# Scores of a seventh pair of heads from unsplit fp32 q and k in a one-core attention and spectral-mixing kernel

## The chip, the cores and the metric

One core of a Trainium2 chip runs the whole program. The metric is device time in microseconds (us), the median of several runs. Lower is better.

## The reference, cut to what matters

Four batches, 12 heads, 448 positions, head size 64, so 768 channels. Causal attention feeds a block that turns its output by learned phases, mixes it along the sequence and projects it.

```python
scores = scale * np.matmul(q, k.transpose(0, 1, 3, 2))      # causal mask, softmax
x = np.matmul(attn, v)                                      # (4, 448, 768) after a transpose
theta = x @ w_theta
zr, zi = x * np.cos(theta), x * np.sin(theta)
y = np.einsum('ts,bsd->btd', w_tok_r, zr) + np.einsum('ts,bsd->btd', w_tok_i, zi)
u = x + y
out = u + np.maximum(u @ w_ch, 0.0)
```

## The kernel before

All matrix products run on TensorE (PE). Most operands are fp32 numbers split into a high and a low fp32r part (a rounded copy and what the copy lost), and a product is the sum of two or three fp32r matmuls. The alternative, one fp32 matmul on the unsplit numbers, shows in the trace as two records per matmul.

Heads are worked in 24 pairs, 6 per batch, pair 0 to 23. For each pair:

- `load_pair` (L383) brings q, k and v. For the first `NQ` pairs (L386) it loads k once into a `kk` buffer and each head's q into one half of the partitions of a zero-padded buffer `QZ` (tiles named `qz`; QZ is a buffer of the rings `zh` and `zl`, two halves used by even and odd pairs). For the other pairs it loads k and q whole (`kr`, `qr`), makes the high part (`copy`, L402, executed by L334 on ScalarE, ACT, or L336 on VectorE, DVE), takes the low part (`alu`, L403, executed at L342), and sends per head two `kk` pieces and two `qs` pieces through DMAs from SBUF to SBUF (L409 and L411).
- `head` (L423) computes per head four score tiles `s` of 448, 336, 224 and 112 columns (matmul L441 for the first NQ pairs, L444 twice for the others), a DVE pass that masks, scales and takes the row minimum (L447), the exponential with its row sums on ACT (L450), and ten 112x112 transposes on PE (L474), which DVE or ACT copies out of PSUM (`p`, L336 or L334).
- After the second head of the pair the row sums are inverted (L457, L458), transposed by PE (L459) into the single PSUM buffer of the ring `xo`, copied out by DVE (`rs`, L460), written to DRAM (`rd`) and read back spread over 64 partitions twice (`rb`). PE then multiplies p and v (L491) into `xo`, and DVE multiplies by `rb` into `xT` (L494). Since `xo` has one buffer, the transposed sums of a pair wait for L494 of the pair before, and the product of p and v waits for L460.

`batch` (L500) follows for each batch: x is split (`xs`, L519 to L523), theta is computed in eight groups of matmuls (L540) into the three PSUM buffers of the ring `m`, DVE takes the fraction of each group (`R`, L562), which frees the buffer, ACT takes sines and cosines, `prep` transposes x and builds the split operands `zh` and `zl`, and `mix` does the sequence mixing (`y`, L620). `project` (L664) and `pair` (L695) do the last product for batches 1 and 2, and for 3 and 0 together. Weights are loaded and split in stages of their own (`weight`, L373, and `decode`, L352): `w_theta` goes to `wth`, `w_tok` to `wtk` during the attention of the first batches.

The order of all instructions is made before the program runs. Each operation has a due time computed from the table `KN` (L22), and `Plan.order` (L97) walks a simple model of the engines: a free engine takes the ready operation with the earliest due time for which buffers are free. Operations with several possible engines (DVE, ACT, GpSimd, which is POOL here) go to the one that is free in the model. So a change of the numbers in KN moves instructions on every engine. All DMAs are issued by one queue, SP, in order; an issue that waits for its data or a buffer holds up all later ones.

```python
def load_pair(pr):
    b, p = divmod(pr, NP)
    t0 = tau(2 * pr)
    if pr < KN["NQ"]:
        kp = buf("kk", [128, 2, S])
```

Of the kernel before, what the change touches and what calls it, by code (L numbers as in the profile page):

```python
# [18 lines left out]
MAGIC = 12582912.0  # L19


KN = dict(S0=-2520.8995, P0=3914.469, P1=7056.6972, V=0.0339, TL=0.8835, RL=-0.0438, SL=7631.8556, SH=2896.8187,  # L22
          LD=2238.5021, LW=-1908.5532, M0=-3353.0467, MR=1.7842, MR2=-0.0229, W0=15032.9046, WT=3030.4005,
          W1=2485.321, WK=2746.2629, E0=-8178.3792, CR=419.9564, O0=2180.1597, OR=0.4535, X0=-265.4206, NS=1, PR=2,
          AE=15377.7073, BB=-1728.1953, AP=5033.1175, AQ=2425.1203, XT=3, NQ=6, WP=2, NW=4, EX=0.4254, PORT=1,
          DW=1450, DE=150, DB=250.0, SL2=0, UL=1823.0792, UD=372.3266, SB=51637.6906, SC=462.9947, XL=-895.2931,
          TS=0.2508, SW=3360.6242, WQ=2)


class Buf:  # L30
# [11 lines left out]
class Plan:  # L42
# [12 lines left out]
    def op(self, eng, dur=None, fn=None, r=(), w=(), lat=None, pr=None, table=None, after=(), port=("POOL",), pen="AP", mode="m"):  # L55
        o = Op()
        o.pen = KN[pen]
        o.port = port
# [38 lines left out]
    def order(self):  # L97
# [3 lines left out]
        def delay(a, b):  # L101
            if b == "PE":
                return 0 if a == "PE" else (310 if a == "POOL" else 365)
            if a == "PE":
                return 197
            if a == "POOL":
                return 102 if b == a else 75
            return 157 if b == "POOL" else 130
# [6 lines left out]
        def turn(a, b):  # L115
            if a == b:
                return 0
            if b == "x":
                return 146
            if a == "x":  # L120
                return 150 if b == "t" else 101
            return 17 if a == "t" and b == "m" else 0
# [28 lines left out]
        while done < len(self.ops):  # L151
# [10 lines left out]
            for e in free:  # L162
# [3 lines left out]
                for o in ready[e]:  # L166
                    if port > t and e in o.port and KN["PORT"]:
                        continue
                    if best is not None and (o.pr > best.pr + KN["SW"] or turn(last[0], o.mode)):
                        continue  # L170
# [23 lines left out]
                if o.wire:  # L194
                    wire = max(wire, fin + KN["DW"]) + o.wire
                    end = wire + KN["DE"]
                out.append((t, o.idx, o))
# [10 lines left out]
                for x in o.succ:  # L208
                    x.n -= 1
                    x.ready = max(x.ready, end + max(delay(e, a) for a in x.alts) + KN["SL2"])  # L210
                    if not x.n:
# [8 lines left out]
def attention_moe_kernel(  # L220
# [42 lines left out]
    def buf(ring, shape, dtype=F32, name=None):  # L263
        def make():
            if ring in ("s", "t", "xo", "m"):
                pool = psum
            elif ring in in_moe:
                pool = moe
            elif ring == "xT":
                pool = xpool  # L270
            elif ring == "rd":
                pool = dram
            elif ring == "ub":
                pool = o_pool[0]
            else:
                pool = apool
            return pool.tile(shape, dtype, tag=ring, name=name or ring, bufs=rings[ring])
        return P.buf(ring, make)
# [35 lines left out]
    def dma(fns, nbytes, r=(), w=(), pr=None, after=(), half=False):  # L314
        def run():
            for f in fns():
                nc.sync.dma_start(out=f[0], in_=f[1])  # L317
        n = nbytes[0]
        o = P.op("SP", 530 if n == 1 else 615.0 * n, run, r, w, lat=0, pr=pr, after=after)
        o.wire = nbytes[1] / KN["DB"]  # L320
        return o
# [3 lines left out]
    def copy(n, o, i, r, w, psum=False, engs=("DVE", "ACT"), after=()):  # L325
        alts = []
        if not psum and P.now <= KN["AE"]:
            engs = tuple(engs) + ("POOL",)
# [10 lines left out]
    def alu(n, o, a, b, op, r, w, engs=("POOL", "DVE"), after=(), pool=False):  # L339
        if P.now > KN["AE"] and not pool:  # L340
            engs = ("DVE",)
        P.op([(e, gp(n) if e == "POOL" else dv(n), lambda e=e: ENG[e].tensor_tensor(out=o(), in0=a(), in1=b(), op=op))  # L342
              for e in engs], r=r, w=w, after=after, port=("POOL", "DVE"))

    def tau(s):
        return KN["S0"] + KN["P0"] * min(s, H) + KN["P1"] * max(s - H, 0)

    def boost(h):
        return KN["BB"] * max(0, h % H - (H - 3)) / 2
# [23 lines left out]
    def weight(src, n, t, i, key, t0, pool):  # L373
        raw = buf("R", [128, 2 * n], I32, "raw")
        z = buf("C", [128, 2, n], F32, "zw")
        dma(lambda: [(raw.t, src.bitcast(I32))], (1, 1024 * n), [], [raw], pr=t0 - KN["LW"])
        P.now = t0
        decode(raw, z, n, lambda: t[:, i, 0], lambda: t[:, i, 1], (key, i), pool)
# [4 lines left out]
# [5 lines that stand above are left out]
            dma(lambda: [(kp.t[:, 0], k[b, p])], (1, 229376), [], [kp], pr=t0 - KN["LD"] - 50000)  # L388
            for hh in range(2):
                own = slice(64 * hh, 64 * hh + 64)  # L390
                qz, i = QZ[hh], pr % 2
                dma(lambda qz=qz, own=own, i=i: [(qz.t[own, i], q[b, p, own])], (1, 114688), [], [(qz, i)],
                    pr=t0 - KN["LD"] + hh - 49999)
                KS[2 * pr + hh], QS[2 * pr + hh] = kp, (qz, i)
        else:
            t1 = t0 - KN["SL"]
            parts = []
            for n, (ring, src) in enumerate((("kr", k), ("qr", q))):
                y = buf(ring, [128, 2, S], F32R)
                dma(lambda y=y, src=src: [(y.t[:, 1].bitcast(F32), src[b, p])], (1, 229376), [], [(y, 0), (y, 1)], pr=t1 - KN["LD"])  # L400
                P.now = t1 + 300 * n
# [12 lines left out]
        vs = buf("vs", [TQ, NJ, 2, D])  # L414
        dma(lambda: [(vs.t, v[b, p])], (1, 229376), [], [vs], pr=t0 - KN["LD"] + 1000)
        VS[pr] = vs
# [6 lines left out]
    def head(h):  # L423
# [42 lines left out]
        for n, js in enumerate(((2,), (3, 1), (0,))):  # L466
            P.now = t0 + per * (KN["TL"] + (1.5, 3, 4)[n] * KN["TS"]) - boost(h)
            pt = buf("t", [TQ, S])
# [366 lines left out]
    for i in range(NTK):  # L835
        weight(w_tok[i], S, wtk, i, bwtk, tau(H) + KN["W1"] + KN["WK"] * i, KN["WP"])
    n_att = len(P.ops)
# [140 lines left out]
```

## Time and profile before

| | |
|---|---|
| median of 3 runs | 484.84 us (483.5 to 486.14) |
| the profiled execution | 482.89 us |
| its span in the profile | 481.1 us |
| busy in the span: PE | 467.7 us (97%) |
| DVE | 396.6 us (82%) |
| ACT | 281.9 us (59%) |
| POOL | 17.6 us (4%) |
| granted clock of PE | 0.998 |

The profiled execution took 1.8 us more than its span; these lie around the span. Busy time is the time in which at least one instruction of the engine is recorded as running. Matmul records overlap their neighbours, so the mean of one record is longer than the time from one matmul to the next.

### The profile page before, as it was taken

To read this page: it belongs to the slowest core of one execution; us is meant where nothing else is said; L and a number is where in the kernel's file an instruction comes from. 1 tells how busy PE (TensorE), PEld (TensorE's weight loads), DVE (VectorE), ACT (ScalarE), POOL (GpSimd) and SP (SyncE) were. 2 spreads that over 40 slices of the span, in tenths; PEclk is the share of its full clock that TensorE was granted. 3 is DMA by queue.
4 is the path that set the end of the run, shared out by engine and by line. 5 is a ranking of instruction groups with operands and counts; after the bars stand their busy time and mean duration, and the time that the engine had idled before them with its cause. 6 is when DMAs were issued, how large, how long until landed. Compare 5 with 4: busy or idle time off the path is not lost.

```text
span 481.1 us, 8541 instructions
## 1 busy us (share of the span) xinstructions
PE 467.7 (97%) x2813; PEld 397.7 (83%) x2813; DVE 396.6 (82%) x1092; ACT 281.9 (59%) x697; POOL 17.6 (4%) x21
## 2 busy tenths in 40 slices
PE   8989899999999999999999999999999999999996
PEld 4655676898887988898888988889798999999995
DVE  4998999879988676898966689984699999968766
ACT  4878689679855455998644659962546722403110
POOL 1202011000000000000000000000000000000000
PEclk9999999999999999999999999999999999999999
DMA  7876787566767576645666664501155200241113
GB/s 240 272 239 192 227 212 201 167 182 172 195 175 199 159 187 164 155 116 154 169 178 143 147 151 136 136 20 53 38 159 148 75 0 20 77 153 38 59 39 134
DMA packets 34651, 68.34 MB, mean 142 GB/s; under 512 B 5680, under 2 KB 24112, under 8 KB 34608
## 3 DMA queue, kind: packets, MB, share of 16 engines
q1 hardware_dynamic: 34608, 67.81, 50.7%
q8 instruction: 22, 0.36, 0.3%
q14 instruction: 21, 0.17, 0.1%
HBM read 36.04 MB, written 6.97 MB: 89 GB/s over the span
## 4 chain that ended last, share of the span: by engine, by line
PE 78%; DVE 11%; DMA 8%; SPq 2%; issue 1%; DVEq 0%
PE y L620 20%; PE th L540 15%; PE cp L682 8%; PE cp L749 8%; PE xo L491 7%; PE t L474 7%; PE s L444 7%; DMA rb<-rd 6%; PE s L441 2%; DVE e L447 2%; SPq L317 2%; PE xp L600 2%; DMA rd<-rs 1%; DVE xT L494 1%; DVE xs L523 1%
## 5 line engine op out<-in xcount | busy, mean ns | idle before, releaser
L450 ACT ACTIVATE e<-e,sm 112x448 f32<-112x448 f32 x192 | 100.5, 524 | 49.1 <-DVE sm L447 47.8
L540 PE MATMUL th<-wth,xs 128*128 128x384 f32 x528 | 111.2, 345 | 1.2 <-DVE R L562 1.1
L447 DVE CUSTOM_DVE_ANT_0 e<-s,mask 112x448 f32<-112x448 f32 x192 | 82.8, 440 | 25.2 <-PE s L444 18.5
L620 PE MATMUL y<-wtk,zh 128*128 128x448 f32 x336 | 98.7, 375 | 0.0
L540 PEld LDWEIGHTS th<-wth,xs 128*128 128x128 f32 x528 | 90.3, 188 | 6.2 <-issue 1.6
L474 PE MATMUL t<-ident,e 112*112 112x112 f32 x480 | 61.9, 260 | 1.9 <-ACT p L334 1.9
L444 PE MATMUL s<-kk,qs 128*112 128x448 f32 (+3 forms) x288 | 63.3, 306 | 0.2
L620 PEld LDWEIGHTS y<-wtk,zh 128*128 128x128 f32 x336 | 58.7, 189 | 3.8
L620 PE MATMUL y<-wtk,zl 128*128 128x448 f32 x168 | 61.3, 365 | 0.0
L474 PEld LDWEIGHTS t<-ident,e 112*112 112x112 f32 x480 | 50.9, 133 | 9.9 <-ACT p L334 2.9
L491 PE MATMUL xo<-p,vs 112*64 112x448 f32 (+3 forms) x384 | 51.0, 406 | 0.0
L444 PEld LDWEIGHTS s<-kk,qs 128*112 128x112 f32 x288 | 47.2, 175 | 4.5 <-DVE sm L447 0.9
L682 PE MATMUL cp<-ub,wa 128*128 128x448 f32 x216 | 46.2, 369 | 0.0
L334 ACT COPY p<-t 112x448 f32<-112x448 f32 (+1 forms) x80 | 35.6, 456 | 15.9 <-PE t L474 15.7
L491 PEld LDWEIGHTS xo<-p,vs 112*64 112x64 f32 x384 | 25.3, 136 | 23.7 <-issue 11.3
L682 PEld LDWEIGHTS cp<-ub,wa 128*128 128x128 f32 x216 | 40.1, 188 | 4.2 <-DVE wa L342 0.6
L336 DVE COPY p<-t 112x448 f32<-112x448 f32 (+1 forms) x64 | 34.1, 542 | 5.0 <-PE t L474 4.8
L450 ACT ACTIVATION_READ_ACCUMULATOR e<-e,sm 112x1 f32 x192 | 36.0, 187 | 0.0
L620 PEld LDWEIGHTS y<-wtk,zl 128*128 128x128 f32 x168 | 31.5, 188 | 2.8
L441 PE MATMUL s<-kk,qz 128*112 128x448 f32 (+3 forms) x96 | 29.3, 419 | 2.1 <-DVE sm L447 1.2
L494 DVE TENSOR_TENSOR xT<-xo,rb 128x448 f32<-128x448 f32 x24 | 14.9, 622 | 18.6 <-PE xo L491 11.1
L441 PEld LDWEIGHTS s<-kk,qz 128*112 128x112 f32 x96 | 14.2, 178 | 10.7 <-DVE sm L447 4.7
(105 smaller groups left out, 616.5 us busy)
## 6 DMA issues: line engine op xcount, KB each, us to landing
kk<-kr SPq DMA_DIRECT2D x72, 224.0 KB
qs<-qr SPq DMA_DIRECT2D x72, 112.0 KB
vs<-v SPq DMA_DIRECT2D x24, 224.0 KB
rb<-rd SPq DMA_DIRECT2D x48, 112.0 KB
raw<-w_theta SPq DMA_DIRECT2D x6, 768.0 KB
rawc<-w_ch SPq DMA_DIRECT2D x12, 384.0 KB
kr<-k SPq DMA_DIRECT2D x18, 224.0 KB
qr<-q SPq DMA_DIRECT2D x18, 224.0 KB
```

The costliest lines, as they stand in the source:

```text
L334: alts.append((e, ac(n, 0 if psum else 1), lambda: nc.scalar.copy(out=o(), in_=i())))
L336: alts.append((e, dv(n) if psum else dv2(n), lambda: nc.vector.tensor_copy(out=o(), in_=i())))
L441: nc.tensor.matmul(out=s.t[:, 0:w], lhsT=qs[0].t[:, qs[1], TQ * j:TQ * j + TQ], rhs=kk.t[:, 0, 0:w])
L444: nc.tensor.matmul(out=s.t[:, 0:w], lhsT=qs.t[:, TQ * j:TQ * j + TQ], rhs=kk.t[:, t, 0:w], start=(t == 0), stop=(t == 1))
L447: P.op("DVE", dv(w) + 8, lambda j=j, w=w, s=s, e=e: nc.vector.tensor_tensor_reduce(out=e.t, in0=s.t[:, 0:w], in1=mask[:, S - w:S], scale=- ...
L450: P.op("ACT", ac(w, 2.5), lambda j=j, e=e: nc.scalar.activation(out=e.t, in_=e.t, func=AF.Exp, scale=-1.0, bias=sm.t[:, 0, hh, j:j + 1], a ...
L474: nc.tensor.transpose(pt.t[:, TQ * n:TQ * n + TQ], E[i].t[:, TQ * j:TQ * j + TQ], ident[0:TQ, 0:TQ])
L491: nc.tensor.matmul(out=xo.t[64 * a:64 * a + 64, TQ * j:S], lhsT=vs.t[:, j, a], rhs=pt(h - 1 + a, j), start=(j == 0), stop=(j == NJ - 1))
L540: nc.tensor.matmul(out=th.t[:, 0:HW], lhsT=l, rhs=wth[:, p, w2, c0:c0 + HW], start=(p == 0 and n == 0), stop=(p == KD - 1 and n == len(ops ...
L620: nc.tensor.matmul(out=y.t[:, 0:S], lhsT=l.t[:, c], rhs=wtk[:, c, w2], start=(c == 0 and n == 0), stop=(c == NTK - 1 and n == 2))
L682: nc.tensor.matmul(out=cp.t[:, 0:S], lhsT=wt()[:, p % NC, w2, 128 * (m % NC):128 * (m % NC) + 128], rhs=us[p].t[:, a], start=(p == 0 and n ...
L749: nc.tensor.matmul(out=banks[m].t[:, 0:S], lhsT=wt()[:, c, w2, 128 * m:128 * m + 128], rhs=ub[c].t[:, a], start=(first and c == 0 and n == 0),
```

## The change

The seventh pair (pair 6, the first pair of batch 1, the second batch) takes the route of the first six: `NQ` goes from 6 to 7. Beside it all due-time numbers of `KN` are new, so the order on all engines is. Nothing else in the program differs. The two lines of the table that name the route:

```diff
-          AE=15377.7073, BB=-1728.1953, AP=5033.1175, AQ=2425.1203, XT=3, NQ=6, WP=2, NW=4, EX=0.4254, PORT=1,
...
+          WK=2001.1803, E0=-6015.5099, CR=152.2681, O0=3470.174, OR=0.2314, X0=-990.0797, NS=1, PR=2, AE=6714.7344,
+          BB=-1147.7937, AP=5199.2148, AQ=3034.4501, XT=3, NQ=7, WP=2, NW=4, EX=-0.0, PORT=1, DW=1450, DE=150,
```

What goes and comes by count. PE: 16 matmuls of L444 go (four of each width), 8 of L441 come (two of each width, each shown as two records). SP: one load of kr, one of qr, four pieces of kk and four of qs go, one load of kk and two of qz come. Splitting of pair 6 goes: two copies and two subtractions. Between engines: DVE takes three subtractions of `wtk` and two casts of `wtk`, two casts of `wth`, three casts of `wa`, and others; POOL and ACT give them up.

**SP, the DMAs around the broadcast `rb` of pairs 2 and 3.** Before (rd_541 and rb_588 are those of pair 2, rd_681 and rb_729 of pair 3, kr_140 and kk of pair 6):

```order
L317 DMA rd_541<-rs_534 8x112
L317 DMA qz_97<-q 64x448
L317 DMA raw_565<-w_tok 128x896
L317 DMA kk_573<-kr_140 64x896 x2
L317 DMA rb_588<-rd_541 64x448 x2
L317 DMA vs_601<-v 112x512
L317 DMA qs_605<-qr_146 64x448 x2
L317 DMA qs_626<-qr_146 64x448 x2
L317 DMA raw_638<-w_tok 128x896
L317 DMA rd_681<-rs_672 8x112
L317 DMA kk_692<-kr_140 64x896 x2
L317 DMA qr_710<-q 128x448
```

After (rd_566 and rb_598 are those of pair 2, rd_680 and rb_708 of pair 3; kr_140 now belongs to pair 7):

```order
L317 DMA rd_566<-rs_562 8x112
L317 DMA raw_575<-w_tok 128x896
L317 DMA rb_598<-rd_566 64x448 x2
L317 DMA vs_612<-v 112x512
L317 DMA raw_623<-w_tok 128x896
L317 DMA qz_103<-q 64x448
L317 DMA rd_680<-rs_672 8x112
L317 DMA rb_708<-rd_680 64x448 x2
L317 DMA vs_721<-v 112x512
L317 DMA raw_727<-w_tok 128x896
L317 DMA qz_97<-q 64x448
L317 DMA kk_739<-kr_140 64x896 x2
```

The pieces of kk that stood between `rd` and `rb` of pairs 2 and 3 are gone; the first of them now stand behind `rb` of pair 3.

**DVE, from the product `xT` of the last pair (23) on.** Before:

```order
L494 TENSOR_TENSOR xT<-xo,rb 128x448
L519 TENSOR_SCALAR xs<-xT 128x128
L336 CAST ub<-xT 128x448
L523 SCALAR_TENSOR_TENSOR xs<-xT,xs 128x128 x2
L342 TENSOR_TENSOR ub<-xT,ub 128x448 x5
L523 SCALAR_TENSOR_TENSOR xs<-xT,xs 128x6x128
L360 TENSOR_SCALAR zc<-rawc 128x384
L562 SCALAR_TENSOR_TENSOR R<-kq,th 128x384
```

After:

```order
L494 TENSOR_TENSOR xT<-xo,rb 128x448
L519 TENSOR_SCALAR xs<-xT 128x128
L336 CAST ub<-xT 128x448
L523 SCALAR_TENSOR_TENSOR xs<-xT,xs 128x128 x2
L342 TENSOR_TENSOR ub<-xT,ub 128x448 x6
L360 TENSOR_SCALAR zc<-rawc 128x384 x2
L364 SCALAR_TENSOR_TENSOR zc<-zc 128x384
L336 CAST wa_4510<-zc 128x384
L342 TENSOR_TENSOR wa_4510<-zc,wa_4510 128x384
L560 TENSOR_SCALAR kq<-th 128x384 x2
L523 SCALAR_TENSOR_TENSOR xs<-xT,xs 128x6x128
L562 SCALAR_TENSOR_TENSOR R<-kq,th 128x384 x2
```

The first `R` (L562), which frees a PSUM buffer of the ring `m`, moved behind seven more instructions (eleven stand between `xT` and `R` before, eighteen now). On PE the work between the last product of p and v (L491) and the matmul that needs that buffer (theta of the third group) changes with it: before it was 9 matmuls of y, 6 of theta and 9 of y; now it is 3 of y, 36 of theta and 15 of y, because 30 matmuls of theta that ran ahead of the product of p and v now run behind it.

**POOL, all that it does behind the constants.** Before:

```order
L826 MEMSET qz 64x448 x2
L331 TENSOR_SCALAR wth<-zw 128x768
L342 TENSOR_TENSOR wth<-zw,wth 128x768 x3
L342 TENSOR_TENSOR wtk<-zw,wtk 128x448 x4
L342 TENSOR_TENSOR ub<-xT,ub 128x448
L342 TENSOR_TENSOR ub<-tt,ub 128x448 x2
```

After:

```order
L826 MEMSET qz 64x448 x2
L342 TENSOR_TENSOR wth<-zw,wth 128x768 x3
L342 TENSOR_TENSOR wtk<-zw,wtk 128x448
L342 TENSOR_TENSOR ub<-xT,ub 128x448
L342 TENSOR_TENSOR ub<-tt,ub 128x448 x2
```

Three subtractions of `wtk` and one copy of `wth` moved from POOL to DVE.

## Rows read from the trace of the kernel before

**Rows 1.** The page, part 4: shares of the chain that ended last, by engine

```profile
PE 78%; DVE 11%; DMA 8%; SPq 2%; issue 1%; DVEq 0%
```

**Rows 2.** Busy time by stretch: length, PE, PEld, DVE, ACT, POOL, clock, DMA

```profile
12.00:91.00 79.00, 73.37 (x459) 51.25 (x458) 73.49 (x244) 61.49 (x180) 11.89 (x8) 1.00 0.77 221
28.00:48.00 20.00, 18.95 (x107) 11.93 (x107) 18.46 (x58) 14.49 (x42) 3.48 (x2) 1.00 0.70 211
...
102.00:340.00 238.00, 237.51 (x1563) 208.68 (x1563) 190.72 (x571) 160.09 (x400) 0.00 (x0) 1.00 0.56 146
```

**Rows 3.** The chain in order of time, 36 to 92 us: start, length, what

```profile
42.12 6.14 DMA rb<-rd
```

**Rows 4.** DVE's waits, 12 to 102 us: total, times, longest

```profile
DVE xT L494 <- DMA rb<-rd: 4.3, 4, 1.9
```

**Rows 5.** DVE in order of time: L494 of pairs 2, 3 and 4, the wait in brackets

```profile
48.36 0.62 DVE L494 TENSOR_TENSOR xT<-xo,rb 128x448 f32<-128x448 f32 x1 [1.90 <-DMA rb<-rd]
...
57.91 0.62 DVE L494 TENSOR_TENSOR xT<-xo,rb 128x448 f32<-128x448 f32 x1 [0.20 <-DMA rb<-rd]
...
67.89 0.62 DVE L494 TENSOR_TENSOR xT<-xo,rb 128x448 f32<-128x448 f32 x1 [0.68 <-DMA rb<-rd]
```

**Rows 6.** SP in order of time: the issues just ahead of rb of pair 2

```profile
40.29 1.14 SPq L317 DMA_DIRECT2D kk<-kr  x2
```

**Rows 7.** Groups by line and shape, PE, score tiles: records, busy us, mean ns

```profile
L444 PE MATMUL s<-kk,qs 128*112 128x448 f32 x72 | 21.0, 373 | 0.0
L444 PE MATMUL s<-kk,qs 128*112 128x336 f32 x72 | 17.6, 325 | 0.0
L444 PE MATMUL s<-kk,qs 128*112 128x224 f32 x72 | 14.1, 277 | 0.1
...
L444 PE MATMUL s<-kk,qs 128*112 128x112 f32 x72 | 12.0, 249 | 0.1
L441 PE MATMUL s<-kk,qz 128*112 128x448 f32 x24 | 12.0, 582 | 1.4 <-DVE sm L447 0.7 <-issue 0.3 <-DMA qz<-q 0.2
L441 PE MATMUL s<-kk,qz 128*112 128x336 f32 x24 | 8.8, 450 | 0.0
...
L441 PE MATMUL s<-kk,qz 128*112 128x224 f32 x24 | 6.9, 370 | 0.6 <-DVE sm L447 0.4
...
L441 PE MATMUL s<-kk,qz 128*112 128x112 f32 x24 | 4.6, 274 | 0.1
```

**Rows 8.** Groups by line, DVE: splitting of kr and of weights, copies of p

```profile
L342 DVE TENSOR_TENSOR kr<-kr 128x448 fp32r<-128x448 f32 x18 | 11.1, 616 | 0.2
...
L336 DVE CAST kr<-kr 128x448 fp32r<-128x448 f32 x10 | 3.9, 388 | 0.3 <-DMA qr<-q 0.2
...
L342 DVE TENSOR_TENSOR wtk<-zw,wtk 128x448 fp32r<-128x448 f32 x3 | 2.1, 703 | 0.0
...
L336 DVE CAST wth<-zw 128x768 fp32r<-128x768 f32 x2 | 1.1, 538 | 0.0
...
L336 DVE COPY p<-t 112x448 f32<-112x448 f32 (+1 forms) x64 | 34.1, 542 | 5.0 <-PE t L474 4.8
```

**Rows 9.** POOL and DVE in order of time, 62.9 to 65.3 us

```profile
62.94 1.90 POOL L342 TENSOR_TENSOR wtk<-zw,wtk 128x448 fp32r<-128x448 f32 x1 [5.35 <-ACT wtk L334]
63.97 1.35 DVE L364 SCALAR_TENSOR_TENSOR zw<-zw 128x448 int32<-128x448 int32 x1
```

**Rows 10.** DVE in order of time, without POOL beside it

```profile
53.36 0.61 DVE L364 SCALAR_TENSOR_TENSOR zw<-zw 128x448 int32<-128x448 int32 x1
```

**Rows 11.** DVE and PE in order of time, behind the last pair's product

```profile
340.86 0.62 DVE L494 TENSOR_TENSOR xT<-xo,rb 128x448 f32<-128x448 f32 x1 [7.26 <-PE xo L491]
...
342.44 2.76 DVE L342 TENSOR_TENSOR ub<-xT,ub 128x448 fp32r<-128x448 f32 x5
...
346.25 0.55 DVE L562 SCALAR_TENSOR_TENSOR R<-kq,th 128x384 f32<-128x384 f32 x1
...
346.86 0.44 PE L540 MATMUL th<-wth,xs 128*128 128x384 f32 x1 [1.09 <-DVE R L562]
```

More of the change, by code (lines that the diff above doesn't have):

```diff
@@ L19 @@
 MAGIC = 12582912.0
-KN = dict(S0=-2520.8995, P0=3914.469, P1=7056.6972, V=0.0339, TL=0.8835, RL=-0.0438, SL=7631.8556, SH=2896.8187,
-          LD=2238.5021, LW=-1908.5532, M0=-3353.0467, MR=1.7842, MR2=-0.0229, W0=15032.9046, WT=3030.4005,
-          W1=2485.321, WK=2746.2629, E0=-8178.3792, CR=419.9564, O0=2180.1597, OR=0.4535, X0=-265.4206, NS=1, PR=2,
-          AE=15377.7073, BB=-1728.1953, AP=5033.1175, AQ=2425.1203, XT=3, NQ=6, WP=2, NW=4, EX=0.4254, PORT=1,
-          DW=1450, DE=150, DB=250.0, SL2=0, UL=1823.0792, UD=372.3266, SB=51637.6906, SC=462.9947, XL=-895.2931,
-          TS=0.2508, SW=3360.6242, WQ=2)
+KN = dict(S0=-2322.2295, P0=3825.9683, P1=7049.4592, V=-0.1301, TL=0.9548, RL=-0.0126, SL=7193.5981, SH=2093.2489,
+          LD=-533.577, LW=-2204.82, M0=-3622.2824, MR=1.7844, MR2=-0.0337, W0=14441.4741, WT=3425.2134, W1=1596.4928,
+          WK=2001.1803, E0=-6015.5099, CR=152.2681, O0=3470.174, OR=0.2314, X0=-990.0797, NS=1, PR=2, AE=6714.7344,
+          BB=-1147.7937, AP=5199.2148, AQ=3034.4501, XT=3, NQ=7, WP=2, NW=4, EX=-0.0, PORT=1, DW=1450, DE=150,
+          DB=250.0, SL2=0, UL=2542.8881, UD=2828.253, SB=239565.2892, SC=460.4297, XL=-486.3376, TS=0.2481,
+          SW=3382.3259, WQ=2)
 class Buf:
```

## The prediction

> **What bounds the kernel now.** I read the shares of the chain first. PE holds 78% of it, DVE 11% and DMAs 8% [rows 1], so this is a PE kernel with something else in part of it. The busy time by stretch shows where. From 102 to 340 us PE is busy 237.51 of 238 us: there the end moves only with PE's work. From 12 to 91 us PE is busy 73.37 of 79 us, so it idles 5.6 us, while DVE is busy 73.49 [rows 2]. Of the rest DVE waits 4.3 us, up to 102 us, for the broadcast `rb` of the inverted row sums [rows 4], in four places. Three are the products of pairs 2, 3 and 4: 1.90, 0.20 and 0.68 us [rows 5], 2.8 us together; 1.5 us falls later. The chain runs through these DMAs as well: the piece for pair 2 counts 6.14 us [rows 3]. So the first 90 us, the front, are set by DVE together with the round trip of the sums. A third place stands late: behind the last pair PE waits 1.09 us for DVE's `R`, which frees a PSUM buffer [rows 11].
>
> So I count what the change does to the length of the front, whether PE can do its added work inside it, and what it does to the late wait. PE's work behind the front is equal but for a few records, and I cost that at nothing. What hides it is that both orders have the same theta and y matmuls ahead of the sums of pair 8; if that were off by a group of three, it would be some 0.6 us.
>
> **PE's added work.** An fp32 tile is two records, and so is a split one. By mean records the extra is 2 x (582 - 373) = 418 ns at 448 columns, 250 at 336, 186 at 224 and 50 at 112 [rows 7]: 0.90 us a head, **1.8 us** for the pair. Taken by the groups' busy time per tile the widest costs 12.0/12 - 21.0/36 = 0.42 us more [rows 7], which is the same. I keep 1.8. These tiles stand in the front. If PE's 5.6 us of idle [rows 2] can hold them, they cost nothing; uncovered, they cost 1.8 in full.
>
> Here a rule bears on the cover. By busy time PE had only 1.05 us free from 28 to 48 us, with 107 matmuls; the full stretch runs 1563 in 238 us, 131 in 20 us [rows 2]. The Trainium skill, Perfetto Trace Analysis, section Identifying the Most-Contended Engine, says that matmul busy time is a poor measure of headroom because matmuls are pipelined, and names the weight-load share instead. The trace agrees, since weight loads are busy 11.93 of 20 us there and 208.68 of 238 later [rows 2]. By that rule the cover is larger, the 0.5 us that I take back below falls away, and the sum would be -3.0 us.
>
> **The broadcast waits.** Between the write of the sums and their broadcast for pair 2, SP had two pieces of kk of pair 6 to issue, 1.14 us of issue alone [rows 6], and their bytes went ahead of `rb`. The new order has none there, and for pair 3 nothing stands between `rd` and `rb`; before, two pieces of kk and a load stood there. Pairs 2, 3 and 4 waited 2.8 us [rows 5]. Bounds: 0 gained (other DMAs fill the place, since DMA was busy 0.77 of the stretch [rows 2]) and 4.3 gained [rows 4]. I take 2.3, all but 0.5 of the three, since the pieces named are the ones that go. What is late next is DVE itself.
>
> **DVE's work.** By the order, up to DVE's copy of pair 6's transposed sums: one subtraction of kr less (0.62), one cast of kr less (0.39), three copies of p less (0.54 each, 1.63), two casts of wth more (0.54 each, 1.08), one cast of wtk more (taken as kr's of the same size, 0.39), two subtractions of wtk more (0.70 each, 1.41) [rows 8] and one L364 step more (0.61) [rows 10]. Sum **+0.9 us**: what pair 6 no longer needs is more than filled by what POOL and ACT give up. As DVE is the bound there I count it in full.
>
> **POOL.** One of POOL's four subtractions of wtk, 1.90 us long, ran beside an L364 of DVE that took 1.35 us [rows 9]; alone it takes 0.61 [rows 10]. So POOL's step cost DVE 0.74 us. Three of these steps leave POOL. I take one such collision back, **-0.7 us**; the bounds are 0 and three, 2.2. The Trainium skill, SBUF — State Buffer, section SBUF: two separate sides, says that POOL and some DVE operations share a port pair under an exclusive lock, and the loser blocks for the whole instruction. The trace agrees for this one pair of rows; by the rule at its strongest, all three would have been collisions, and the sum would be -4.0 us.
>
> **Does it fit?** The front shortens by 2.3 - 0.9 + 0.7 = 2.1 us and PE has 1.8 more to do in it: 3.9 of the 5.6 us of idle. That fits, but tightly, and a PE that waits in order never uses all of its idle. I take 0.5 back: **-1.6 us** for the front.
>
> **The late wait.** Before, PE did 24 matmuls from 340.86 to 345.77 us (the wait of 1.09 taken off 346.86), 0.205 us each, and `R` ended at 346.80 [rows 11]. By the new order PE has 3 + 36 + 15 = 54 matmuls to do first: 11.1 us, to 351.9 on the same scale. `R` stands behind seven more DVE instructions; at 0.55 us, as the five subtractions show (2.76 us), that is 3.9 us, so it ends at 350.7 [rows 11]. The buffer is free about a microsecond early. Bounds: the wait stays (0) or goes (-1.09). I take **-0.9**. What hides `R` is the theta work moved behind the last product; if DVE were 1 us later, the wait would be back.
>
> **Sum.** -1.6 - 0.9 = **-2.5 us**. The profiled execution took 482.89 us (span 481.1 and 1.8 around it), so 480.4 against it. That execution stood 1.95 us below the median of the runs shown, 484.84, and the same step from the median gives **482.3 us**, which is my number. Some 0.5%, 2.4 us, is about what a measurement of this kernel can tell from no change, so the forecast lies just at that edge.
>
> **Rivals.**
> *The front gives all it can.* Every wait for rb goes (4.3) [rows 4] and POOL's three steps were three collisions (2.2) [rows 9]. Then PE is the limit: its idle of 5.6 [rows 2] less 1.8 of new work leaves 3.8, and with 1.1 late the time falls 4.9 us, to 479.9. For it: nothing else of weight stands in that stretch. Against: DVE, 93% busy there [rows 2], would have to run without a gap. The lock named above is the page's part in this. Chance 0.17.
>
> *The front does not move.* The relief is spent elsewhere. The new order puts a load of v, which has to wait for the product of p and v of the same pair, ahead of the broadcasts of pair 1 and of pair 6, and the raw weights still go between. If that costs DVE the 2.3 us again, and 0.5 of the rest, the front is worth 0 to +0.5, the late wait -0.9: -0.9 to -0.4, or 484.2. Chance 0.18.
>
> *Slower: the score tiles of pair 6 come late to DVE.* DVE works in order, the front is DVE's, and each of the eight tiles arrives 0.05 to 0.42 us later [rows 7]. If DVE stands at each, it loses 1.8 us, and its added work of 0.9 comes on top: +2.7, with no gain from rb, since DVE waits for tiles and not for rb. With -0.9 late that is +1.8, 486.6; with the late wait still there +2.7, 487.5. It decides from the point where PE is less than half a microsecond ahead of DVE when these tiles start. Against it: the tiles of pairs 0 to 5 went the same way, and PE idles there. Chance 0.20.
>
> **How the numbers follow.** The forecast, -1.2 to -4.0 us, has 0.45; 0.27 of that lies beyond 0.5%. With the first rival faster has 0.44. The second rival, the rest of the forecast and 0.06 of the third make 0.42 for the same. The third leaves 0.14 for slower. The range goes from a little beyond the first rival, 479.5, to nearly the end of the third, 487.2.
>
> **What would show it.** Right: from 12 to 91 us DVE waits for rb under 1 us, PE's idle falls to about 2 us though eight fp32 tiles more lie in it, PE becomes full 1 to 2 us earlier, and behind the last product theta of the third group starts without a wait. Wrong: DVE waits for score tiles of pair 6, or for rb of pairs 1 and 6; a new PE wait in the full stretch; or POOL's steps gone without any DVE step growing shorter. If the time rises by more than 2 us, cover was what I had wrong.

## The result, and the profile after

The changed kernel took 480.04 us (median of 4 runs, 478.42 to 480.27), the kernel before 484.96 beside it (4 runs, 483.5 to 486.14): a ratio of **0.989 [0.986, 0.993]**, or 4.9 us less. The forecast was 2.5 us less, 482.3. In 87 further runs of the kernel before, beside the experiments, the median was 484.27 us; against these the gain is 4.2 us. The profiled execution took 478.42 us with a span of 476.6, so 4.5 us less than the one of before.

First the chain of the changed kernel, by engine:

```profile
PE 85%; DVE 10%; DMA 2%; issue 1%; ACT 1%; SPq 0%; DVEq 0%; ACTq 0%
```

DMA went from 8% of the chain [rows 1] to 2%, and PE took its place. In the front, from 12 to 91 us, the broadcast, the write of the sums (`rd`) and SP's issues were 45% of the chain; in the changed kernel none of the three is among the shares shown, and PE's matmuls lead. First before, then after (the view cuts its line at the end):

```profile
by line: DMA rb<-rd 27.6%; DVE e L447 10.0%; DMA rd<-rs 9.0%; SPq L317 8.4%; PE s L441 6.4%; DVE xT L494 4.9%; issue 4.8%; DVE zw L360 4.1%; PE t L474 3.9%; DVE zw L364 3.8%; DVE p L336 2.6%; PE xo L491 2.6%; DVE R L562 1.8%; DVE xs L523 1.
```

```profile
by line: PE s L441 16.2%; PE th L540 15.9%; PE xo L491 13.1%; PE t L474 11.0%; DVE e L447 8.3%; DVE zw L360 5.8%; DVE zw L364 4.3%; PE s L444 4.2%; issue 4.1%; DVE p L336 3.1%; ACT e L450 1.9%; DVE wtk L342 1.8%; DVE xT L494 1.4%; DVE wth L
```

Then the busy time by stretch (length, PE, PEld, DVE, ACT, POOL, clock, DMA share and GB/s):

```profile
12.00:91.00 79.00, 77.20 (x483) 54.89 (x481) 76.81 (x259) 64.19 (x190) 7.11 (x4) 1.00 0.71 209
28.00:48.00 20.00, 19.00 (x121) 12.65 (x119) 20.00 (x63) 15.69 (x46) 1.83 (x1) 1.00 0.68 210
0.00:102.00 102.00, 98.09 (x593) 69.31 (x594) 89.06 (x308) 77.08 (x224) 9.33 (x14) 1.00 0.73 212
336.00:350.00 14.00, 14.00 (x78) 13.50 (x77) 11.21 (x26) 4.07 (x8) 0.00 (x0) 1.00 0.35 91
```

And the same for the kernel before, where its section has no row:

```profile
0.00:102.00 102.00, 94.67 (x568) 65.91 (x569) 86.69 (x296) 74.62 (x218) 14.12 (x18) 1.00 0.76 219
336.00:350.00 14.00, 12.90 (x75) 11.01 (x74) 9.10 (x21) 6.85 (x14) 0.00 (x0) 1.00 0.19 55
```

PE's idle time from 12 to 91 us fell from 5.6 us [rows 2] to 1.8, and DVE is busy every moment from 28 to 48 us (18.46 of 20 before). Up to 102 us PE did 25 matmul records more. DVE's longest waits from 12 to 102 us in the changed kernel (total, times, longest):

```profile
DVE kq L560 <- PE th L540: 2.1, 1, 2.1
...
DVE e L447 <- PE s L441: 0.5, 1, 0.5
DVE e L447 <- PE s L444: 0.4, 2, 0.3
```

The line for `rb`, 4.3 us before [rows 4], isn't there any more. DVE in order of time shows the products L494 of pairs 2, 3, 4 and 18 in the changed kernel, none with a wait for `rb`:

```profile
46.19 0.60 DVE L494 TENSOR_TENSOR xT<-xo,rb 128x448 f32<-128x448 f32 x1
...
54.08 0.62 DVE L494 TENSOR_TENSOR xT<-xo,rb 128x448 f32<-128x448 f32 x1
...
65.58 0.61 DVE L494 TENSOR_TENSOR xT<-xo,rb 128x448 f32<-128x448 f32 x1
...
260.18 0.63 DVE L494 TENSOR_TENSOR xT<-xo,rb 128x448 f32<-128x448 f32 x1 [0.34 <-PE xo L491]
```

and the fourth `rb` wait of before, at pair 6, and its pair 18:

```profile
89.48 0.62 DVE L494 TENSOR_TENSOR xT<-xo,rb 128x448 f32<-128x448 f32 x1 [1.54 <-DMA rb<-rd]
...
264.18 0.63 DVE L494 TENSOR_TENSOR xT<-xo,rb 128x448 f32<-128x448 f32 x1 [0.34 <-PE xo L491]
```

Against the rows of before [rows 5] pair 2 is 2.2 us earlier, pair 3 3.8, pair 4 2.3 and pair 6 (now at 85.86) 3.6. At pair 18 it is 4.0. So **nearly the whole gain is made in the front**, and it is carried through the stretch in which PE is full (the shift of a single product also depends on its place in the new order, so it doesn't tell at which pair the time is won). Why `rb` is in time shows on SP's queue around pair 2, first before, then after (start, length, what is issued):

```profile
37.88 0.29 SPq L317 DMA_DIRECT2D rd<-rs  x1
...
41.52 1.70 SPq L317 DMA_DIRECT2D rb<-rd  x2
```

```profile
39.11 0.29 SPq L317 DMA_DIRECT2D rd<-rs  x1
39.81 0.34 SPq L317 DMA_DIRECT2D raw<-w_tok  x1
40.40 1.69 SPq L317 DMA_DIRECT2D rb<-rd  x2
```

From the write of the sums to the end of the broadcast's issue it was 5.3 us (37.88 to 43.22) and is 3.0 (39.11 to 42.09); the two pieces of kk of [rows 6] are not there. From that write to the product it was 10.5 us and is 7.1. At pair 3 the issue ends 2.4 us after the write, for 4.0 before. These two pairs had 2.1 of the 4.3 us of waits.

The other 2.2 us, at pairs 4 and 6, went in another way. At pair 6, before and then after:

```profile
81.21 0.43 SPq L317 DMA_DIRECT2D rd<-rs  x1
...
85.97 1.20 SPq L317 DMA_DIRECT2D rb<-rd  x2
```

```profile
76.90 0.29 SPq L317 DMA_DIRECT2D rd<-rs  x1
...
81.84 1.10 SPq L317 DMA_DIRECT2D rb<-rd  x2
```

From the write to the end of the broadcast's issue it is 6.0 us both times, and at pair 4 it is even 5.6 us for 5.0. But the product comes later behind the write, 9.0 us for 8.3 at pair 6 and 9.8 for 8.7 at pair 4: the new order has seven more DVE instructions between the copy of the sums and the product, at both pairs. There DVE has other work to do while the broadcast is under way.

Late, PE works without a gap from 336 to 350 us: the wait of 1.09 us behind the last product [rows 11] is gone. But a new one came up at 364.61, in PE's order of time, for an `R` that DVE reached only at 364.01:

```profile
364.61 0.55 PE L600 MATMUL xp<-ident,xT 128*128 128x128 f32 x3 [0.74 <-DVE R L562]
```

So the late part gave 1.09 - 0.74, about 0.4 us. The front gave 4.0 of the 4.5 between the two profiles.

### The profile page after: what moved, and what is told of

Read it like the earlier page. It is cut to its first block, busy times and chain, and to the rows that moved or that the text cites. A ratio compares the mean times of both kernels' runs of the same rounds, so it can differ in the third digit from the quotient of the medians.

```text
span 476.6 us, 8528 instructions
## 1 busy us (share of the span) xinstructions
PE 467.1 (98%) x2813; PEld 397.3 (83%) x2813; DVE 401.1 (84%) x1107; ACT 276.2 (58%) x682; POOL 12.8 (3%) x17
## 4 chain that ended last, share of the span: by engine, by line
PE 85%; DVE 10%; DMA 2%; issue 1%; ACT 1%; SPq 0%; DVEq 0%; ACTq 0%
PE y L620 21%; PE th L540 17%; PE xo L491 9%; PE cp L682 9%; PE cp L749 8%; PE t L474 8%; PE s L444 7%; PE s L441 4%; DVE e L447 2%; PE xp L600 1%; DVE zw L360 1%; DMA kk<-kr 1%; DVE zw L364 1%; DMA kr<-k 1%; DVE p L336 1%
## 5 line engine op out<-in xcount | busy, mean ns | idle before, releaser
L474 PE MATMUL t<-ident,e 112*112 112x112 f32 x480 | 63.2, 260 | 0.9 <-ACT p L334 0.9
L444 PE MATMUL s<-kk,qs 128*112 128x448 f32 (+3 forms) x272 | 59.1, 301 | 0.6 <-DVE sm L447 0.6
L491 PE MATMUL xo<-p,vs 112*64 112x448 f32 (+3 forms) x384 | 51.0, 406 | 0.0
L444 PEld LDWEIGHTS s<-kk,qs 128*112 128x112 f32 x272 | 45.6, 175 | 4.0 <-DVE sm L447 0.9
L491 PEld LDWEIGHTS xo<-p,vs 112*64 112x64 f32 x384 | 25.3, 136 | 24.7 <-issue 13.2
L441 PE MATMUL s<-kk,qz 128*112 128x448 f32 (+3 forms) x112 | 34.9, 417 | 1.6 <-DMA qz<-q 0.6
L334 ACT CAST zh<-C 128x512 fp32r<-128x512 f32 x19 | 11.8, 620 | 25.6 <-DVE C L603 19.6
L441 PEld LDWEIGHTS s<-kk,qz 128*112 128x112 f32 x112 | 16.0, 176 | 10.7 <-DVE sm L447 5.4
```

The costliest lines, as they stand in the source:

```text
L334: alts.append((e, ac(n, 0 if psum else 1), lambda: nc.scalar.copy(out=o(), in_=i())))
L441: nc.tensor.matmul(out=s.t[:, 0:w], lhsT=qs[0].t[:, qs[1], TQ * j:TQ * j + TQ], rhs=kk.t[:, 0, 0:w])
L444: nc.tensor.matmul(out=s.t[:, 0:w], lhsT=qs.t[:, TQ * j:TQ * j + TQ], rhs=kk.t[:, t, 0:w], start=(t == 0), stop=(t == 1))
L474: nc.tensor.transpose(pt.t[:, TQ * n:TQ * n + TQ], E[i].t[:, TQ * j:TQ * j + TQ], ident[0:TQ, 0:TQ])
L491: nc.tensor.matmul(out=xo.t[64 * a:64 * a + 64, TQ * j:S], lhsT=vs.t[:, j, a], rhs=pt(h - 1 + a, j), start=(j == 0), stop=(j == NJ - 1))
```

## The experiments

Theory: the front is DVE's, and DVE waited for `rb` because the bytes and issues for pair 6's split k and q stood ahead of it; PE's idle time pays for the fp32 tiles, and is then used up. Rivals: the new order alone did it; POOL's steps did it; PE or DVE alone sets the front. The ratios are to the kernel before, run beside each.

### The route without the new order, and the new order without the route

```diff
- (kernel before)  NQ=6
+ NQ=7
```

> The numbers of before with NQ=7 alone; the order is planned again from the old numbers. Theory (the pieces of pair 6 ahead of the broadcasts are what cost the front): most of the gain is here, 2 to 4 us below before, and DVE's wait for rb from 12 to 102 us is under 1.5 us against 4.3. Rival (the new order made the gain, the route alone costs PE's 1.8 us): between 1 us faster and 2 us slower, and DVE still waits 3 us or more for rb.

Measured: 482.41 us, ratio 0.996 [0.994, 0.999], so 1.7 us faster where the theory gave 2 to 4. DVE's waits from 12 to 102 us, in a profile that is the slowest of the twelve runs (486.46 us, mean granted clock 0.993):

```profile
DVE e L447 <- PE s L441: 2.7, 4, 1.1
DVE e L447 <- PE s L444: 1.5, 3, 0.8
DVE xT L494 <- DMA rb<-rd: 1.0, 3, 0.6
```

With the old numbers, the route alone takes 3.3 of the 4.3 us of `rb` waits away, and in this profile DVE waits 4.2 us for score tiles instead. They are not the tiles of pair 6, of which the third rival speaks. The last wait for a tile of L441 in this stretch is this one:

```profile
60.16 0.62 DVE L447 CUSTOM_DVE_ANT_0 e<-s,mask 112x448 f32<-112x448 f32 x1 [0.30 <-PE s L441]
```

Pair 6's tiles are computed from 68.46 to 79.32 us, and L444 computes those of pair 7 and later. The two longest waits for L441, 1.03 and 1.10 us, end at 37.23 and 53.09 us, just behind or inside stretches in which PE's granted clock was 0.73 to 0.84, so how much of them a run at full clock has stays open.

```diff
- (changed kernel)  NQ=7
+ NQ=6
```

> The new numbers with the old route, NQ=6; the order is planned again from the new numbers. Theory: 2 to 4 us of the 4.9 are lost again, with pieces of pair 6 ahead of rb of pairs 2 and 3 and DVE waiting for rb by 2 us or more. Rival (the order made the gain): as fast as the changed kernel within 1 us, or up to 1.7 us faster since PE has less to do.

Measured: 488.85 us, ratio 1.009 [1.007, 1.012]. The new numbers with a split pair 6 are slower than either kernel, and lose 8.8 us where 2 to 4 were expected. The wait expected isn't there: DVE has no wait for `rb` in this stretch. It waits for other things:

```profile
DVE zw L360 <- DMA raw<-w_tok: 4.3, 1, 4.3
DVE e L447 <- PE s L444: 3.9, 5, 2.2
DVE xs L519 <- PE th L540: 3.2, 2, 1.9
```

The gain isn't a sum of two gains: -0.4% for the route, +0.9% for the numbers, -1.1% for both. With the pieces of pair 6 back on the queue a raw weight is late, and score tiles of later pairs. In all six runs the mean granted clock was down too (0.988 to 0.993), so a part of the loss may be the clock's.

### Bytes ahead of rb

In the kernel before, the pieces of kk of pair 6 behind `rb` of pairs 2 and 3, SP's order alone:

```diff
+        for tag, ref in ((("kk", 6, 0), ("rb", 2)), (("kk", 6, 1), ("rb", 3))):
+            behind(tag, ref)
```

> The kernel before with one thing moved on SP: the two kk pieces of each head of pair 6 are issued behind the broadcast rb of pair 2 and of pair 3 and not ahead of them. Nothing moves on the other engines. Theory: DVE's waits of 1.90 and 0.20 us at pairs 2 and 3 fall to under 0.6 together and the time falls by 1 to 1.5 us. Rival (the bytes are only shifted, DVE then waits for the later tiles or broadcasts): the wait moves to pair 3, 4 or to a score tile of pair 6 and the time stays within 0.5 us.

Measured: 483.39 us, ratio 0.999 [0.996, 1.002]; DVE's wait for `rb` (L503 there) from 4.3 to 3.0:

```profile
DVE xT L503 <- DMA rb<-rd: 3.0, 3, 2.0
```

The waits at pairs 2 and 3, 2.1 us, are gone, as the theory had it, but those of pairs 4 to 6 grew by 0.7, as the rival had it. A shorter wait and no time that can be measured. The next run went further: everything that stood between the write of the sums and the broadcast of pairs 2, 3 and 4 put behind it.

```diff
+            late = [o for o in order[i + 1:j] if o.eng == "SP"]
+            order[i:j + 1] = [o for o in order[i:j + 1] if o not in late] + late
```

> The kernel before, with everything that SP issues between the write of the sums and their broadcast for pairs 2, 3 and 4 (loads of q and of raw weights, pieces of kk and qs) moved to just behind the broadcast; only SP's order changes. Theory (bytes and issues ahead of rb make DVE wait, and that wait is the front's length): DVE's waits for rb up to 102 us fall from 4.3 us to under 1.5 us and the time by 1.5 to 2.8 us, ratio 0.994 to 0.997. Rival 1 (the pieces that are now late make a new wait: kk of pair 6 or raw weights): rb's waits fall, DVE's waits for score tiles or for raw rise by as much, ratio 0.999 to 1.003. Rival 2 (the rb trip is long by itself): the waits stay over 3 us, ratio 1.000.

Measured: 488.9 us, ratio 1.009 [1.006, 1.012]. Rival 1 held, and cost more than I had priced: `rb`'s waits (L501) fall to 1.9 us, but raw weights come late. The profile is the slowest of the six runs (491.58 us), and all six had a mean granted clock of 0.996 or less, so a part of the loss may be the clock's.

```profile
DVE zw L364 <- DMA raw<-w_tok: 4.9, 2, 2.9
...
DVE xT L501 <- DMA rb<-rd: 1.9, 1, 1.9
```

SP's rows around pair 4 show what a broadcast directly behind its write can cost:

```profile
61.16 0.29 SPq L321 DMA_DIRECT2D rd<-rs  x1
64.89 1.11 SPq L321 DMA_DIRECT2D rb<-rd  x2
66.10 1.18 SPq L321 DMA_DIRECT2D qs<-qr  x2
```

For 3.4 us, until the sums have landed, SP issues nothing. At pairs 2 and 3 of the same run this wait is 1.0 and 0.9 us, so 3.4 is the worst of three. The pieces between were useful filling as long as there was as much to move. So these two changes of SP's order alone bought no time. In every order that was run with the pieces of pair 6 on the queue something was late for DVE: `rb` by 2.2 to 4.3 us, or a raw weight by 4.9 or, with the new numbers, 4.3. In the changed kernel, which has less to move, neither is.

The opposite test, in the changed kernel: two needless DRAM-to-DRAM copies of 224 KB ahead of `rb` of pairs 2 and of 3.

```diff
+            if o.tag in (("rb", 2), ("rb", 3)):
+                for i in range(2):
+                    nc.sync.dma_start(out=junk[2 * (o.tag[1] - 2) + i], in_=v[3, 2 * (o.tag[1] - 2) + i])
```

> The changed kernel with two loads of 224 KB each put ahead of the broadcast rb of pair 2 and of pair 3 (copies of v from DRAM to DRAM, which nobody reads), about the bytes and the number of issues that stood there before. Theory: DVE waits for rb again, 1 to 2.5 us over the two pairs, and the time rises by 1 to 2.5 us. Rival (the front has slack in DVE's new order): DVE's waits for rb stay under 0.5 us and the time within 0.5 us.

Measured: 482.06 us, ratio 0.996 [0.993, 0.999]; some 2 us of the gain are gone, and there are waits again (L504 and L365 there):

```profile
DVE xT L504 <- DMA rb<-rd: 3.3, 2, 1.7
...
DVE zw L365 <- DMA raw<-w_tok: 1.4, 1, 1.4
```

Of the 3.3 us, 1.52 stand at pair 2, behind the copies, none at pair 3, and 1.75 at pair 6, some 39 us behind the last copy. A wait of 1.46 us at pair 6 shows in the run with doubled fp32 tiles below, too, which adds no bytes, so this half need not be the copies' own.

### Is PE's added work covered?

Pair 6's score tiles computed twice, in the kernel before (split tiles) and in the changed one (fp32 tiles; both replace a result by itself).

```diff
- (kernel before)                 for t in range(2):
+                for t in (0, 1, 0, 1) if pr == 6 else (0, 1):
```

> The kernel before with the eight split score tiles of pair 6 computed twice (the second result replaces the first), nothing else moved: more PE work in the front, no DVE work, no DMA. By the trace of before a pair of split tiles is 1.8 us of busy time a head, so at most 3.6 us more on PE. Theory of the prediction (DVE and the rb trips set the front, PE's 5.6 us of idle covers added work): 0 to +0.7 us, ratio 0.999 to 1.002, PE's busy time from 12 to 91 us up by 2 to 3 us, no new PE wait behind it. Rival (PE's idle is no cover, each late tile makes DVE late): +2 to +3.6 us, ratio 1.004 to 1.008, with DVE waits for score tiles of pair 6.

Measured: 483.74 us, ratio 1.000 [0.998, 1.002]. Covered. PE's busy time from 12 to 91 us rose by 0.7 us (73.37 to 74.08), less than the 2 to 3 expected.

```diff
- (changed kernel)  one matmul for each tile
+                    for _ in range(2 if pr == 6 else 1):
```

> The changed kernel with the eight fp32 score tiles of pair 6 computed twice, nothing else moved. More PE work than in the other kernel of this kind: at most 5.4 us of busy time, at least the 1.8 us by which fp32 tiles exceed split ones. In the changed kernel PE has only 1.8 us of idle left from 12 to 91 us. Theory (the cover is used up, the front of the changed kernel is near the limit of both engines): +2 to +4 us against the changed kernel, so a ratio to the kernel before of 0.993 to 0.998. Rival (DVE alone sets the pace, PE's work stays covered): the ratio stays at 0.989 to 0.991.

Measured: 482.78 us, ratio 0.997 [0.996, 0.999]. The kernel of the late wait, below, which is the changed one but for the place of one instruction, took 480.16 us in the same comparison, so these tiles cost 2.6 us. In the trace PE, by stretch, is no fuller than in the changed kernel:

```profile
12.00:91.00 79.00, 76.88 (x474) 53.67 (x472) 73.37 (x247) 61.83 (x181) 7.13 (x4) 1.00 0.69 209
```

DVE's busy time there falls from 76.81 to 73.37 us. It waits 2.4 us for score tiles, 1.8 of it for those of pair 6, which is the mechanism of the third rival, and 1.5 us for `rb` of pair 6. So doubled tiles were free before and are paid after. The two additions aren't equal, though: by the busy times in [rows 7] eight more split tiles are at most 3.6 us, eight more fp32 tiles at most 5.4, and a part of the difference may be that. Going one pair further asks the same question.

```diff
- (changed kernel)  NQ=7
+ NQ=8
```

> The changed kernel's numbers with eight unsplit pairs instead of seven: one step more in the same direction, another 1.9 us of PE work (8 tiles), less splitting on DVE, ACT and SP; the planner makes a new order from the same numbers. Theory (PE's cover is used up: 1.8 us of idle left from 12 to 91 us): +1 to +2.5 us against the changed kernel, ratio to the kernel before 0.991 to 0.995. Rival (what DVE no longer splits is worth as much as for pair 6): 0.986 to 0.989. A new order made from numbers that were not found for it may also cost more by waits that have nothing to do with pair 7; those would show as PE waits of over 1 us for DVE or for a load of q.

Measured: 480.77 us, ratio 0.993 [0.991, 0.996]: a ratio inside what the theory gave, but only 0.7 us above the changed kernel's median, and not to be told apart from its ratio, 0.989 [0.986, 0.993]. What can be said is that an eighth pair brings no further gain. Its profile has a wait of PE for `qz` at the start, 1.4 us for 0.6 in the changed kernel; the run with doubled split tiles has 1.3, so it need not belong to pair 7.

### Is there room on DVE?

A needless instruction of about 0.6 us behind the copy of the sums of pairs 2 to 5, in both kernels.

```diff
+                if b == 0 and pr in (2, 3, 4, 5):
+                    nc.vector.tensor_tensor(out=mask, in0=mask, in1=mask, op=ALU.max)
```

> The kernel before with the same four useless DVE instructions at the same places, just ahead of the products that wait for rb. Theory (DVE waits there for rb in any case: 1.90, 0.20 and 0.68 us for pairs 2, 3 and 4): the instructions of 0.6 us are hidden at pairs 2 and 4 and in part at 3, so 0 to +1.2 us, ratio 1.000 to 1.0025, and the waits for rb fall by 1 to 1.5 us. Rival (the waits named in the trace are not what sets the length): +2.4 us, ratio 1.005, with the waits for rb as long as before.

> The changed kernel with one useless DVE instruction (the mask's maximum with itself, 112 x 448, about 0.6 us) just behind the copy of the transposed sums of each of pairs 2, 3, 4 and 5: 2.4 us of DVE work, nothing for PE. Theory (DVE is full there, 20.00 of 20 us from 28 to 48, and no wait is left that would hide it): +1.8 to +2.6 us against the changed kernel, ratio to the kernel before 0.993 to 0.995. Rival (PE alone sets the front now): 0.989 to 0.991.

Measured: before with them 486.36 us, ratio 1.004 [1.002, 1.007]; after with them 480.81, ratio 0.994 [0.992, 0.996]. In the kernel before the wait for `rb` fell by 2.1 us (4.3 to 2.2), but 1.35 of it at pair 6 (1.54 to 0.19), where no instruction was added:

```profile
DVE xT L498 <- DMA rb<-rd: 2.2, 3, 1.5
```

Yet the median rose by 2 us, against the expectation. A reason shows in the stretches of that profile, the slowest of the twelve (488.5 us):

```profile
44.00:48.00 4.00, 3.29 (x20) 1.94 (x16) 4.00 (x11) 0.49 (x1) 0.00 (x0) 1.00 0.92 258
48.00:52.00 4.00, 2.75 (x8) 1.47 (x9) 2.21 (x8) 3.86 (x14) 1.81 (x1) 0.79 0.94 248
52.00:56.00 4.00, 4.00 (x24) 3.62 (x23) 3.63 (x17) 3.15 (x11) 0.00 (x0) 0.78 0.26 77
```

PE idles 0.7 and then 1.25 us of 4, and its granted clock is 0.79 in the second of these stretches and 0.78 in the next. Five of this kernel's twelve runs, with a mean clock of 0.997 or over, had a median of 484.36 us; the seven below had 487.58. In the runs of the unchanged kernel beside them it was 483.91 and 484.87. So where the clock held, the four instructions cost some 0.5 us, as the theory had it, and where it fell some 2.7. In the changed kernel no run fell so, and the 2.4 us cost 0.8 us by the medians (480.04), 1.2 by the product of pair 18 in the two profiles (260.18 to 261.40) and 2.2 by the ratios (0.989), for 1.8 to 2.6 expected. Some of it is paid; how much stays open, and that DVE alone sets the pace of the changed front isn't shown.

### POOL's steps

Three of POOL's four subtractions of wtk put on DVE at the same places, in the kernel before:

```diff
+        moved = [o for o in order if o.tag == ("low", S) and o.eng == "POOL"][1:]
+        for o in moved:
+            o.run = o.alts["DVE"][1]
```

> The kernel before with three of POOL's four subtractions of wtk done by DVE at the same place of the order. DVE gets three subtractions of 0.70 us more, 2.1 us, in the stretch that it bounds, and loses what POOL's steps cost it beside them. By the prediction's term one collision of 0.7 us goes: +1.4 us, ratio 1.003. If all three were collisions (2.2 us): 0, ratio 1.000. If POOL's steps cost DVE nothing: +2.1 us or more, ratio 1.004 to 1.006. In the trace: L364 steps of 1.35 us beside POOL before; here all at 0.6 us.

Measured: 483.65 us, ratio 1.000 [0.998, 1.003]. The groups on DVE up to 102 us, before and then here, for the step that was stretched (L364, here L368) and the subtractions (L342, here L346):

```profile
L364 DVE SCALAR_TENSOR_TENSOR zw<-zw 128x448 int32<-128x448 int32 x7 | 4.9, 713 | 0.1
...
L342 DVE TENSOR_TENSOR wtk<-zw,wtk 128x448 fp32r<-128x448 f32 x3 | 2.1, 703 | 0.0
```

```profile
L368 DVE SCALAR_TENSOR_TENSOR zw<-zw 128x448 int32<-128x448 int32 x7 | 4.2, 610 | 0.0
L346 DVE TENSOR_TENSOR wtk<-zw,wtk 128x448 fp32r<-128x448 f32 x6 | 3.7, 610 | 0.0
```

L364 gets 0.7 us shorter in all, the three old subtractions 3 x 0.09 = 0.3: the three steps had cost DVE 1.0 us. Each mean hides a single long row: the L364 of 1.35 us [rows 9], and this subtraction beside POOL's next step (72.8 to 73.9 us):

```profile
73.54 0.87 DVE L342 TENSOR_TENSOR wtk<-zw,wtk 128x448 fp32r<-128x448 f32 x1
```

Beside POOL's last step (81.7 to 82.8 us) no DVE row is longer. Three new subtractions add 1.8 us, and the waits for `rb` take up the rest (4.3 to 3.1). So the time stays the same, where the prediction's term gave +1.4 us. No change is what was expected if all three steps were collisions, but it came in another way: one collision, a part of a second, and a wait that hid the remainder.

### The late wait

In the changed kernel, the `R` that PE waits for issued two DVE instructions earlier:

```diff
+        dve = [n for n in range(ir) if order[n].eng == "DVE"][-2:]
+        order.insert(max(dve[0], ik + 1), order.pop(ir))
```

> The changed kernel with one DVE instruction of the last batch, the R (L562) of the third group's second half, issued two places earlier, ahead of a copy of C and an L364 step. Theory: PE's new wait of 0.74 us for this R at 364 us goes, and the end comes 0.5 to 0.75 us earlier than in the changed kernel: ratio to the kernel before about 0.988 (0.9893 for the changed kernel). Rival: the DVE step that is passed (L364 of wa) is then late for the PE work that follows, and the wait only moves: 0.9893, with a PE wait of 0.3 us or more for wa or C between 364 and 370 us.

Measured: 480.16 us, ratio 0.992 [0.990, 0.994]: no faster than the changed kernel. PE's rows show the rival at work. The wait for `R` is gone, and PE waits for the halves of `wa` that now come later, 0.95 us in two pieces:

```profile
365.60 0.67 PE L689 MATMUL cp<-ub,wa 128*128 128x448 f32 x2 [0.69 <-DVE wa L340]
366.53 0.67 PE L689 MATMUL cp<-ub,wa 128*128 128x448 f32 x2 [0.26 <-DVE wa L346]
```

Around 364 us DVE has both `R` and the decoding of `w_ch` in one queue, and this change of order only moved the wait. None of the experiments came out faster than the changed kernel.

## Why the prediction was right, and where it was too small

**What bounds the kernel.** Right for the kernel before. The front was DVE's together with the broadcast's trip; less to wait for moved the whole rest of the kernel by 4.0 us without a loss. In the changed kernel the front's chain runs through PE for the greater part (the five PE shares shown make 60%), so the bound has moved. Three of the signs named came: no wait for `rb`, PE's idle at 1.8 us, and no wait for theta of the third group.

**The broadcast waits** were the term that was mis-sized: -2.3 us forecast. I took the pieces of kk at pairs 2, 3 and 4, all but 0.5 of 2.8 us, and kept 4.3 as the far bound, because I looked for named pieces between a write and its broadcast. All 4.3 us went; with 4.3 for 2.3, and nothing taken back, the sum for the front is 4.1 us, and 4.0 was measured. My mechanism holds for pairs 2 and 3, 2.1 us: there the trip got shorter. At pairs 4 and 6, 2.2 us, it didn't; there DVE's new order has more work ahead of the product, at which I hadn't looked. Of the waits the run with the route alone took away 3.3 us and gained 1.7, the run that only moved the named pieces took away 1.3 and gained nothing measurable, and the run that moved all of them to behind the broadcast lost 4.5 us. The new numbers with the pieces still on the queue have no wait for `rb` either, but others. So neither the place of the pieces nor the order alone makes the gain; it came where the pair's loads, four pieces of kk and four of qs were off the queue and the order was new. How the 4 us divide between the two stays open.

**PE's added work**, 1.8 us covered by 5.6 of idle: right. Doubled split tiles were free in the kernel before, and doubled fp32 tiles cost 2.6 us in the changed one, so the cover was there, and the change used up at least the greater part of it.

**"Take back 0.5".** The step was wrong in sign: PE gave more than its idle time. Up to 102 us idle fell from 7.3 to 3.9 us (102 less 94.67 and 98.09), by 3.4. Yet the 25 further records, at the 0.15 us of the full stretch (237.51 us for 1563) [rows 2], are an estimated 3.8 us of work, and pair 6's longer tiles another 1.8. So by this estimate some 2 us came out of time in which PE counted as busy. The Trainium skill, Perfetto Trace Analysis, section Identifying the Most-Contended Engine, says that matmul busy time is no good measure of the room left, and these 2 us agree; the sum that I left aside, -3.0 us, was the better one. The weight-load share that it names doesn't tell whether added matmuls are free, though: it was 54.89 of 79 us in the changed front, 69%, and doubled tiles cost 2.6 us there, with 2.4 us of DVE's waits for tiles.

**POOL**, -0.7 us: right, one collision as taken. In the changed kernel as in the run on POOL the seven L364 steps fell from 713 to some 610 ns, 0.7 us. The rule of the Trainium skill on the shared port (SBUF — State Buffer, section SBUF: two separate sides) at its strongest, three collisions of 0.74 us, isn't borne out: the three steps of POOL cost DVE 0.74, 0.26 and 0 us, 1.0 together.

**DVE's work**, +0.9 us, can't be read by itself. DVE is at 20.00 of 20 us, but that added work counts in full in the front isn't shown: of 2.4 us put there in the changed kernel 0.8 to 2.2 were paid.

**The late wait**, -0.9 forecast, -0.4 measured. The third group's theta found its buffer free, as worked out. But I followed only that one `R`: a later one came 0.74 us after PE wanted its buffer. DVE has the decoding of `w_ch` in the same queue there, and the run that moved this `R` only moved the wait.

**The rivals.** The first, "the front gives all it can", came out at the measured time, 479.9 against 480.04, but by luck, with parts that hold only by half: all of `rb`'s waits went, but POOL's steps were not three collisions and the late wait wasn't worth 1.1. The second is refuted by the shift of pair 18; the load of v that it named did stand ahead of `rb` of pair 6, until 81.42 us, and no wait of DVE came of it. The mechanism of the third shows in one run, where pair 6's fp32 tiles are computed twice and DVE waits 1.8 us for them. In the changed kernel DVE waits 0.9 us for score tiles in the front, 0.5 of it for the last tile of pair 5, the rest behind pair 6 and none at pair 6.

## What to carry to other kernels

A wait of one engine for a small transfer went here with fewer transfers on that queue and a new order of that engine's work; reordering the queue alone bought nothing, and while SP stood directly behind the round trip it issued nothing, for 0.9 to 3.4 us. A resource with idle time can buy off work from a full one until its idle is gone, and doubling one piece of work in both kernels helps to tell whether that point has come. When a wait disappears, look at both sides of it: whether what was waited for came sooner, or who waited came later. When a late wait is followed up, follow it to the next buffers of the same ring, and to what else is in that engine's queue.

## What the runs showed of the hardware

The clock was a second price that I hadn't thought of. In four of the experiments' profiles (the two on the route and the numbers, the broadcast put first, and the needless DVE work in the kernel before) PE's gaps in the front were followed by stretches at a lower granted clock. The kernel that put the broadcast first, by stretches of 4 us:

```profile
72.00:76.00 4.00, 1.54 (x9) 1.18 (x7) 0.42 (x1) 1.13 (x3) 0.00 (x0) 1.00 1.03 227
76.00:80.00 4.00, 2.83 (x10) 1.20 (x12) 2.61 (x6) 4.00 (x14) 0.48 (x1) 0.53 0.53 124
80.00:84.00 4.00, 4.00 (x27) 2.98 (x24) 2.38 (x10) 2.45 (x8) 0.66 (x1) 0.62 0.76 216
84.00:88.00 4.00, 3.56 (x25) 2.59 (x25) 3.83 (x18) 3.91 (x15) 0.00 (x0) 1.00 0.25 88
```

PE idled 2.5 us of the first stretch and 1.2 of the second; the granted clock was then 0.53 to 0.62, so most of the time the lower of the two levels, 1.2 GHz, and full again in the stretch after those. The kernel before had such a fall in some of its runs: of its 87 runs beside the experiments 34 had a mean granted clock under 0.997, against none of the 46 runs of the changed kernel and of its versions with an eighth pair, doubled tiles, needless DVE work or the moved `R`. With bytes put ahead of `rb` again it was 5 of 12. This bears on a part of the measured gain that the two profiles (0.998 each) don't show. The 53 runs of the kernel before at 0.997 or over had a median of 483.59 us and all 87 one of 484.27, so some 0.7 us of the 4.2 go with the clock, and some 3.5 are left without it. In the profile of the kernel before PE has gaps of 0.73 and 1.23 us around the product of pair 2 (45.1 and 47.8 us), and the changed kernel has none there; that these gaps make the difference is not shown.
